# Re-planned start of a two-stage kernel: wide fillers, weights between the first units, paired score matmuls, VectorE kept off GpSimd's time

## The chip, the cores and the metric

The kernel runs on one NeuronCore of a Trainium2 chip. The metric is the device time of one execution in microseconds. It has TensorE (PE; its weight loads are listed apart as PEld), VectorE (DVE), ScalarE (ACT), GpSimd (POOL) and SyncE (SP), which issues nearly all DMAs here. A tensor of up to 128 partitions is worked on at a time; matmul results go to PSUM, which has eight banks.

## What is computed

The reference is a linear attention with a decaying state, followed by a two-layer network:

```python
for t in range(S):                       # B, H, S, D = 4, 8, 768, 48
    cur = einsum('bhd,bhe->bhde', u * k[t], v[t])
    y[t] = einsum('bhd,bhde->bhe', r[t], state + cur)
    state = w * state + einsum('bhd,bhe->bhde', k[t], v[t])
x = y as (3072, 384)                     # tokens x (heads * head size)
h = x @ w_in                             # 384 -> 2048
g = where(h >= 1, h, where(h <= -1, 0, (h + 1)**2 / 4))
out = g @ w_out                          # 2048 -> 384, float32
```

All inputs and the output are float32. The kernel computes g as the square (h/2 + 1/2)^2 alone, and finds from norms of x and of the columns of w_in whether any h could leave -1..1; a flag then sends it into a slower branch, which the given inputs do not take.

## The kernel before, in words

The time axis is cut into 6 chunks of 128 steps. One chunk of one batch is a **unit**: 24 units, chunk by chunk, so that units 0 to 3 are the first chunk of the four batches and need no earlier state. Each unit goes through these steps (lines of the kernel before):

- three loads K, R, Vf of 192 KB (L383, issued by SP);
- K and R times powers of the decay, to bfloat16 (`kw` L447, `rw` L451), and V to bfloat16 (`v`);
- a transpose: for units 0 to 7 eight matmuls (`tr` L469, or four and four as `trk` and `trr` for units 0 and 1) and a copy out of PSUM (`rk`), for the others a transposing DMA (`trd` L488);
- scores: eight matmuls into two PSUM banks (`at` L499) and two masked copies on VectorE (`mask` L505);
- the diagonal term: `P`, `dg`, `dc` for units 0 to 7, or `ku` on GpSimd and `red`; then `vd`;
- `y` L556 and L559, the sum `x` on VectorE (L571), its transpose to xT (`xp` L581 and `xt`, or `xtd` by DMA), and the sum of squares `x2` (L597);
- the state: `st` on TensorE (L607), `t`, `tw`, `bd`.

Two units make a **block** m of 256 tokens, 12 in all. Layer 1 of a block is eight pieces `L1_m_n` (six matmuls of 256 columns, L644), each ended by a ScalarE square `g` (L656) into a bfloat16 tile; layer 2 of a unit is four pieces `L2_i_s` (four matmuls of 384 columns, L667), an evacuation and a store (L690). Piece s of layer 2 needs the s-th quarter of w_out; pieces of layer 2 follow one another strictly, and so do those of layer 1. The weights come as four quarters of w_in (I0 to I3) and four of w_out (O0 to O3), 768 KB each (L419), every one converted to bfloat16 in slices that VectorE, ScalarE and GpSimd share.

The order on each engine is not written by hand. Every operation is handed to a planner (class `Plan`) with its cost on each allowed engine, what it depends on, which buffers it takes, and a due time; `run` plays them through and emits each engine's instructions in the resulting order. On the chip an engine works its list in order and waits at its head. Due times are made of a list per block (`CFG["due"]`, `CFG["step"]`) and a bias per kind. `CFG["order"]` gives the order of the first loads. Where TensorE has nothing else before a set time, the planner lets it run **fillers** `wm` (L357): two matmuls of 128 columns on zeros.

The attention part shares four PSUM banks (pool "a"), layer 1 has two ("h"), layer 2 two ("o").

Of the kernel before, what the change touches and what calls it, by code (L numbers as in the profile page):

```python
# [14 lines left out]
SEM = 0.06  # L15
CFG = {
    "order": "U0 U1 U2 U3 I0 I1 I2 I3 O0 O1 O2 U4 O3 U5 U6 U7",
    "soft": 8,
    "sw": False,
    "due": [12.12, 22.15, 27.93, 36.84, 35.31],  # L20
    "step": 12.04,
    "warm": 24.0,
    "steady": 45.0,
    "slack": 0.19,
    "split": 2,
    "bias": {
        "at": 1.0, "bd": -4.91, "c_uw": 1.38, "dg": 0.1, "ku": -0.0, "kw": 1.96, "ldVf": 1.45, "red": -0.75,
        "rk": 0.3, "rkk": -6.72, "rkr": -0.29, "rw": 1.99, "st": 0.57, "t": -0.92, "trd": 0.24, "trk": -2.87,
        "trr": -3.35, "tw": -0.9, "v": -0.89, "x2": -1.05, "xt": 2.62, "y": -2.02,
# [4 lines left out]
class Buf:  # L34
    def __init__(self, pool):
        self.pool, self.users, self.slot, self.t = pool, [], None, None


class Op:
    def __init__(self, name, engs, fn, deps, uses, allocs, due, dma, after, nb, late):  # L40
        self.name, self.engs, self.fn, self.due, self.dma = name, engs, fn, due, dma
        self.after, self.nb, self.late = [a for a in after if a], nb, late
        self.deps, self.uses, self.allocs = [d for d in deps if d], list(uses), list(allocs)
        self.eng = self.start = self.end = None
        for b in self.uses + self.allocs:
            b.users.append(self)


class Plan:
# [13 lines left out]
    def place(self, o):  # L63
        got, t = [], 0.0
        for b in o.allocs:
            best = None
            for i, cur in enumerate(self.slots[b.pool]):
                if any(g[0] == b.pool and g[1] == i for g in got):
                    continue
                if cur is None:  # L70
                    free = 0.0
                elif all(u.start is not None for u in cur.users):
                    free = max(u.end for u in cur.users) + SEM
                else:
                    continue
                if best is None or free < best[0]:
                    best = (free, i)
            if best is None:
                return None
            got.append((b.pool, best[1]))  # L80
            t = max(t, best[0])
        return t, got

    def run(self):
# [5 lines left out]
        while todo:  # L90
            cand, gone = [], []
            for o in todo:
                if any(d.start is None for d in o.deps) or any(a.start is None for a in o.after):
                    if o.late is not None and free["PE"] > o.late:
                        gone.append(o)
                    continue
# [15 lines left out]
            for o in gone:  # L112
                todo.remove(o)
                for b in o.uses:
                    b.users.remove(o)
            if not cand and gone:
                continue
            if not cand:
                raise RuntimeError("no operation can be placed: " + ", ".join(o.name for o in todo[:12]))
# [16 lines left out]
            occ, lat = o.engs[e]  # L136
            o.eng, o.start = e, est
            for b, (p, i) in zip(o.allocs, pl):
                b.slot = i
                self.slots[p][i] = b  # L140
            if o.dma is not None:
# [4 lines left out]
                begin = max(served, issue + wait)  # L146
                served = begin + took
                ring.append((served, nd))
                free[e] = issue
                o.end = served + 0.6 + (1.0 if est > steady else 0.0)  # L150
# [7 lines left out]
            todo.remove(o)  # L158
            done.append(o)
        done.sort(key=lambda o: o.start)  # L160
# [27 lines left out]
def kernel(  # L188
# [28 lines left out]
    NS = CFG["soft"]  # L217
    D_m = list(CFG["due"])
    while len(D_m) < NB + 2:
# [11 lines left out]
        "x": 5, "x2": 2, "g": 5, "os": 3, "sq": 2, "ss": 2,  # L231
    }
    P = Plan(slots)
    rows = rot.tile([1, 2, H, DP], F32, name="rows", tag=f"g_{slots['g'] - 1}")

# [15 lines left out]
    u_row = const.tile([1, H * D], F32, name="u_row")  # L251
    zero = const.tile([128, 128], BF16, name="zero")
    onesf = const.tile([1, 128], F32, name="onesf")
    w_row = const.tile([1, H * D], F32, name="w_row")
    wc = const.tile([128, NP], F32, name="wc")
    ident = const.tile([128, 128], BF16, name="ident")
    umask = const.tile([128, 128], F32, name="umask")
    ones = const.tile([128, 1], BF16, name="ones")
# [9 lines left out]
    xT = [const.tile([128, nKb, MT], BF16, name=f"xT{m}") for m in range(NB)]  # L268
    xn = const.tile([128, NU], F32, name="xn")
    wsq = const.tile([128, nN], F32, name="wsq")  # L270
# [7 lines left out]
    wc3 = wc[:, :, None].to_broadcast([128, NP, D])  # L278
    umask4 = umask[:, None, :].to_broadcast([128, NP, 128])
# [14 lines left out]
    c_wr = P.op("c_wr", {"ACT": (0.4, 0)}, lambda e: nc.scalar.dma_start(out=w_row, in_=row(w)), due=-100, dma=(0.05, 1, 0.6))  # L294
    c_ur = P.op("c_ur", {"ACT": (0.4, 0)}, lambda e: nc.scalar.dma_start(out=u_row, in_=row(u)), after=[c_wr], due=-99.5, dma=(0.05, 1, 0.6))
    c_ubc = P.op("c_ubc", {"SP": (0.4, 0)}, lambda e: nc.sync.dma_start(out=u_bc, in_=row_bcast(u)), due=D_m[NS // UB] - 25, dma=(0.7, 8, 0.6))
# [21 lines left out]
    c_um = P.op("c_um", {"POOL": (0.6, 0.7)}, f_um, due=-97)  # L318
# [8 lines left out]
    c_lrow = P.op("c_lrow", act(384, False), lambda e: nc.scalar.activation(rows[:, 0, :, 0:D], heads(w_row), AF.Ln), deps=[c_wr, c_rz], due=-98)  # L327
    c_urow = P.op("c_urow", dve(384), lambda e: nc.vector.tensor_mul(rows[:, 1, :, 0:D], heads(w_row), heads(u_row)), deps=[c_wr, c_ur, c_rz], due=8.5)
    lwb = Buf("a")

    def f_lwb(e):
        get(lwb, [128, H, D], F32)
        mm(lwb.t, onesf, rows[:, 0, :, 0:D], start=True, stop=True)
    c_lw = P.op("c_lw", pe(1.3), f_lwb, deps=[c_lrow, c_z], allocs=[lwb], due=-98)
    colb = Buf("a")

    def f_colT(e):
        get(colb, [128, 2, NP], F32)
        for i in range(2):
            for p in range(NP):  # L340
                nc.tensor.transpose(colb.t[:, i, p : p + 1], rows[:, i, 2 * p : 2 * p + 2, :].rearrange("q h d -> q (h d)"), onesf[:, 0:1])
    c_colT = P.op("c_colT", pe(0.5), f_colT, deps=[c_lrow, c_urow], allocs=[colb], due=9)
    c_wc = P.op("c_wc", {"ACT": (0.15, 0.2)}, lambda e: nc.scalar.activation(wc, colb.t[:, 0, :], AF.Exp, scale=float(C)), deps=[c_colT], uses=[colb], due=10)

    def f_uw(e):
        for s in range(2):
            nc.vector.tensor_copy(uw[halves[s], :, s], colb.t[halves[s], 1, :])
    c_uw = P.op("c_uw", {"DVE": (0.3, 0.35)}, f_uw, deps=[c_colT, c_z], uses=[colb], due=9)
# [3 lines left out]
    for i in range(160):  # L352
        def f_wm(e, i=i):
            if wmb.t is None:
                get(wmb, [128, 128], F32)
            for _ in range(2):
                mm(wmb.t, zero, zero, start=True, stop=True, skip_group_check=True)  # L357
        wm0 = P.op(f"wm{i}", pe(0.22 if i < 18 else 0.11), f_wm, deps=[c_z], uses=[wmb] if i else [], allocs=[] if i else [wmb], after=[wm0] if i else [], due=2000.0, late=CFG["warm"] if i else None)
    c_winv = P.op("c_winv", act(384), lambda e: nc.scalar.activation(Winv, lwb.t, AF.Exp, scale=negj_col), deps=[c_lw, c_icol], uses=[lwb], due=-97)
# [453 lines left out]
```

## Time and profile before

| | |
|---|---|
| median of 9 runs | 182.01 us (180.2 to 183.54) |
| the profiled execution | 180.22 us, of which its span is 178.2 us |
| TensorE busy | 168.0 us (94%) |
| VectorE, ScalarE, GpSimd busy | 111.3, 116.1, 105.1 us |
| first piece of layer 1 begins | 18.48 us |
| last quarter of w_out converted, first piece that needs it | 36.95, 37.00 us |
| last matmul ends | 172.30 us |
| DMA | 31.50 MB, mean 177 GB/s over the span |

The page cuts the span into 40 slices of 4.455 us; a digit is the busy share in tenths. Matmuls are pipelined, so the duration of a matmul is longer than the room that it takes; the distance from the start of one group to the start of the next tells that room where TensorE is never idle. Times inside the span count from its start.

### The profile page before, as it was taken

Reading aid. Unit: us, or ns where it says so; the run is one execution under the profiler, and the core shown is the slowest. Engines: PE = TensorE matmul, PEld = TensorE weight load, DVE = VectorE, ACT = ScalarE, POOL = GpSimd, SP = SyncE. Lnnn points to the kernel's source line nnn. Section 1 sums busy time; section 2 is a strip of 40 time slices with the busy share of each in tenths; the row PEclk is TensorE's granted clock in tenths of the full one; section 3 lists DMA queues with packets and bytes.
Section 4 is the critical chain, followed back from the end, with each engine's and each line's share of the span. In section 5 each row is a group of like instructions: output and inputs, shape, how many; then the busy total and the mean of one; then the engine's idle time right before and its main releaser. Section 6 shows DMA issues by size and latency. Waiting matters only on the chain.

```text
span 178.2 us, 4705 instructions
## 1 busy us (share of the span) xinstructions
PE 168.0 (94%) x1808; PEld 127.0 (71%) x1808; DVE 111.3 (62%) x221; ACT 116.1 (65%) x257; POOL 105.1 (59%) x142
## 2 busy tenths in 40 slices
PE   7899959999999999999999999999999999999960
PEld 7689947867768777777777777777767777777730
DVE  6799955399899796678667865757676444100000
ACT  4359967744756986875886885967685556554510
POOL 8658563187895999796599669579775600000000
PEclk9999999999999999999999999999999999999996
DMA  5999999999989968969979989799898962111111
GB/s 113 209 174 283 394 349 340 264 179 196 179 193 186 207 133 171 218 142 206 188 166 168 204 173 197 197 181 216 162 188 157 241 167 70 22 44 48 44 60 45
DMA packets 105920, 31.50 MB, mean 177 GB/s; under 512 B 98978, under 2 KB 104356, under 8 KB 105892
## 3 DMA queue, kind: packets, MB, share of 16 engines
q1 hardware_dynamic: 105744, 31.04, 79.6%
q8 instruction: 16, 0.26, 0.6%
q14 instruction: 12, 0.10, 0.2%
q10 hardware_dynamic: 148, 0.10, 0.2%
HBM read 20.65 MB, written 4.72 MB: 142 GB/s over the span
## 4 chain that ended last, share of the span: by engine, by line
PE 72%; DMA 11%; SPq 8%; DVE 4%; issue 1%; POOL 1%; ACT 0%; ACTq 0%; DVEq 0%
PE o L667 33%; PE h L644 29%; DMA wf<-in_moe_w_out_dram 11%; SPq L383 6%; PE a L499 3%; SPq L419 3%; PE a L559 2%; PE a L556 2%; PE a L607 1%; DVE AT L505 1%; POOL w_out_sb L284 1%; DVE x L571 1%; PE a L469 1%; DVE VD L546 0%; PE a L581 0%
## 5 line engine op out<-in xcount | busy, mean ns | idle before, releaser
L644 PE MATMUL h<-xT,w_in_sb 128*128 128x256 bf16 x576 | 77.8, 273 | 1.8 <-DVE w_in_sb L284 1.4
L667 PE MATMUL o<-w_out_sb,g 128*128 128x384 bf16 x384 | 77.0, 326 | 0.2 <-POOL w_out_sb L284 0.2
L656 ACT ACTIVATE g<-h 128x512 bf16<-128x512 f32 x96 | 56.6, 595 | 28.3 <-PE h L644 27.1
L644 PEld LDWEIGHTS <-w_in_sb 128*128 128x128 bf16 x576 | 54.4, 98 | 15.6 <-DVE w_in_sb L284 1.6
L667 PEld LDWEIGHTS <-g 128*128 128x128 bf16 x384 | 35.2, 98 | 15.8 <-issue 0.2
L505 DVE TENSOR_TENSOR AT<-a,umask 128x512 bf16<-128x512 f32 x48 | 31.1, 684 | 7.6 <-PE a L499 7.4
L546 POOL TENSOR_TENSOR VD<-V,dg 128x384 f32<-128x384 bf16 x18 | 15.7, 873 | 12.1 <-DVE dg L541 6.3
L571 DVE TENSOR_TENSOR x<-a,VD 128x384 bf16<-128x384 f32 x24 | 13.3, 554 | 12.0 <-PE a L559 10.5
L536 POOL TENSOR_TENSOR KU<-KU,R 128x384 f32<-128x384 f32 x16 | 17.7, 1109 | 3.6 <-DMA R<-in_r_dram 2.5
L451 DVE TENSOR_TENSOR KR<-R,Wpow 128x384 bf16<-128x384 f32 x20 | 17.6, 879 | 3.3 <-DMA R<-in_r_dram 3.3
L535 POOL TENSOR_TENSOR KU<-K,u_bc 128x384 f32<-128x384 f32 x16 | 18.4, 1150 | 0.1
L597 ACT ACTIVATE x<-x 128x384 bf16<-128x384 bf16 x24 | 12.5, 522 | 5.4 <-DVE x L571 5.1
L284 DVE COPY os<-o 128x384 f32<-128x384 f32 (+1 forms) x6 | 3.1, 523 | 20.3 <-ACT os L284 18.7
L618 POOL TENSOR_TENSOR T<-T,wc 128x192 f32<-128x192 f32 x20 | 11.9, 596 | 5.0 <-ACT T L284 3.6
L357 PE MATMUL o<-zero 128*128 128x128 bf16 x156 | 13.0, 236 | 1.0 <-DVE zero L321 1.0
L447 POOL TENSOR_TENSOR KR<-K,Winv 128x384 bf16<-128x384 f32 x11 | 11.0, 997 | 3.6 <-DMA K<-in_k_dram 2.8
L284 ACT COPY os<-o 128x384 f32<-128x384 f32 (+1 forms) x19 | 8.9, 469 | 6.3 <-PE o L667 4.0
L614 DVE TENSOR_TENSOR T<-T,a 48x192 f32<-48x192 f32 x32 | 11.1, 348 | 2.3 <-PE a L607 1.7
L284 ACT CAST V<-Vf 128x384 bf16<-128x384 f32 x19 | 9.6, 507 | 4.1 <-DMA Vf<-in_v_dram 3.9
L284 ACT CAST Tbd<-T 48x192 bf16<-48x192 f32 x30 | 10.4, 347 | 2.0 <-PE a L556 1.2
L357 PEld LDWEIGHTS <-zero 128*128 128x128 bf16 x156 | 10.6, 107 | 1.2 <-DVE zero L321 1.0
L447 DVE TENSOR_TENSOR KR<-K,Winv 128x384 bf16<-128x384 f32 x13 | 9.5, 727 | 2.5 <-DMA K<-in_k_dram 2.4
(78 smaller groups left out, 173.1 us busy)
## 6 DMA issues: line engine op xcount, KB each, us to landing
K<-in_k_dram SPq DMA_DIRECT2D x24, 192.0 KB, 3.8
R<-in_r_dram SPq DMA_DIRECT2D x24, 192.0 KB, 4.4
Vf<-in_v_dram SPq DMA_DIRECT2D x24, 192.0 KB, 4.2
out_dram<-os SPq DMA_DIRECT2D x23, 192.0 KB, 2.4
wf<-in_moe_w_in_dram SPq DMA_DIRECT2D x4, 768.0 KB, 8.5
wf<-in_moe_w_out_dram SPq DMA_DIRECT2D x4, 768.0 KB, 8.5
RK<-KR SPq DMA_TRANSPOSE x16, 3.2
xT<-x SPq DMA_TRANSPOSE x16, 3.1
```

The lines of the kernel that those rows point to most:

```text
L284: (nc.scalar.copy if eng == "ACT" else V_ENG[eng].tensor_copy)(o, i)
L357: mm(wmb.t, zero, zero, start=True, stop=True, skip_group_check=True)
L447: V_ENG[e].tensor_mul(krb.t[:, H:, 0:D], Kb.t, Winv)
L451: V_ENG[e].tensor_mul(krb.t[:, :H, 0:D], Rb.t, Wpow)
L505: nc.vector.tensor_mul(atb.t[s], at_p[s].t, umask4)
L535: nc.gpsimd.tensor_mul(kub.t, Kb.t, u3)
L536: nc.gpsimd.tensor_mul(kub.t, kub.t, Rb.t)
L546: V_ENG[e].tensor_mul(vdb.t, vb.t, dgb.t[:, :, None].to_broadcast([128, H, D]))
L571: nc.vector.tensor_add(xb.t, yb.t[:, 0:384].rearrange("p (h d) -> p h d", h=H), vdb.t)
L644: mm(hb.t[:, f, :], w_in_sb[:, kk, (2 * n + f) * 128 : (2 * n + f + 1) * 128], xT[m][:, kk, :], start=(kk == 0), stop=(kk == nKb - 1),)
L656: nc.scalar.activation(gb[m].t[:, 2 * n : 2 * n + 2, :], hb.t, AF.Square, bias=0.5, scale=0.5)
L667: mm(ob.t, gb[m].t[:, f, j * C : (j + 1) * C], w_out_sb[:, f, :], start=(f == 0), stop=(f == nN - 1))
```

## The change

The planner's order of the first loads, its model and several operations change; the mathematics does not.

- **Loads.** I0 now comes after unit 0's K and R and I1 after unit 1's; w_out's first three quarters are no longer mixed with unit 4's loads. The row w is loaded first, on SP's queue.
- **Decay tables.** w is spread over 128 partitions by two matmuls and then taken to its logarithm; before, the logarithm came first.
- **Fillers.** One matmul of 256 columns in place of two of 128.
- **Planner.** Matmuls that start before 9.0 us are counted twice as long; some VectorE operations are made to wait, in the plan, for GpSimd; all biases and due times are new.
- **Blocks 0 and 1.** Layer 1 works on one unit (128 columns) at a time, twelve matmuls in a piece, so that a piece needs only its own unit's xT.
- **Units.** Units 0 to 3 transpose in two halves (`split`), units 8 and 9 transpose by TensorE too, `at` of both units of a block is one operation of 16 matmuls from block 5 on, one mask of units 0 and 1 goes through ScalarE, and units 0 and 1 may use all PSUM pools.
- **Norms of w_in.** One matmul group at the end in place of eight small ones; one buffer for the squares in place of two.
- **End.** The last unit's layer 2 is 256 columns and then 128 in a PSUM bank of its own, each stored from SP; some stores of units 12 to 17 are split in two so that the number of DMAs is a multiple of 8. The branch that is not taken becomes a loop.

```diff
-    "order": "U0 U1 U2 U3 I0 I1 I2 I3 O0 O1 O2 U4 O3 U5 U6 U7",
-    "soft": 8,
+    "order": "U0 I0 U1 I1 U2 U3 I2 I3 O0 O1 O2 U4 O3 U5 U6 U7",
+    "tpe": 10, "dmm": 8, "xpe": 8, "pair": 5, "cold": 9.0, "fine": 2,
+    "am0": 0, "am1": 2, "norm": 100.0, "wide": 2,
...
+            if e == "DVE" and o.sb and free["POOL"] > est + 0.15:
+                occ, lat = occ + free["POOL"] - est - 0.15, lat + free["POOL"] - est - 0.15
+            if e == "PE" and est < CFG["cold"] and o.name[:2] != "wm":
+                occ, lat = 2.0 * occ, lat + occ
...
-        "x": 5, "x2": 2, "g": 5, "os": 3, "sq": 2, "ss": 2,
+        "x": 5, "x2": 2, "g": 5, "os": 3, "sq": 1, "ss": 2, "am": 2,
...
+    c_wr = P.op("c_wr", {"SP": (0.5, 0)}, lambda e: nc.sync.dma_start(out=w_sp[0:128:64, :], in_=w.rearrange("(s h) d -> s (h d)", s=2)), due=-1000, dma=(0.05, 1, 0.5))
...
+    def f_wb(e):
+        for s in range(2):
+            get(wbb[s], [128, H // 2, D], F32)
+            mm(wbb[s].t, onesf[s * DP : s * DP + 1, :], w_sp[s * DP : s * DP + 1, :], start=True, stop=True)
+    def f_lw(e):
+        for s in range(2):
+            nc.scalar.activation(lw[:, lws[s]], wbb[s].t, AF.Ln)
...
-            for _ in range(2):
-                mm(wmb.t, zero, zero, start=True, stop=True, skip_group_check=True)
+            mm(wmb.t, zero[:, 0:128], zero, start=True, stop=True, skip_group_check=True)
...
+        A = "a h o" if i < CFG["wide"] else "a"
+        by_pe, by_mm, x_pe = i < CFG["tpe"], i < CFG["dmm"], i < CFG["xpe"]
...
+                def f_am(e, s=s, amb=amb):
+                    get(amb, [128, NP, 128], BF16)
+                    nc.scalar.copy(amb.t, at_p[s].t)
...
+    for m in range(NB):
+        gens = [attention(UB * m + j) for j in range(UB)]
+        got = [next(g) for g in gens]
+        if m >= CFG["pair"]:
+            def f_at2(e, got=got):
+                for x in got:
+                    x[0](e)
+            o = P.op(f"at_{m}", pe(0.63), f_at2, deps=got[0][1] + got[1][1], uses=[x[2] for x in got], allocs=got[0][3] + got[1][3], due=got[0][4])
...
+            if fine:
+                get(hb, [128, 4, C], F32)
+                parts = [(f, 4 * q + f, slice(j * C, (j + 1) * C)) for f in range(4)]
...
-        parts = [(0, d_out)] if i < NU - 1 else [(0, d_out // 2), (d_out // 2, d_out)]
+        cuts = [(0, d_out)] if i < NU - 1 else [(0, 256), (256, d_out)]
+        rows_ = [(0, C)] if i not in TWICE else [(0, C // 2), (C // 2, C)]
+        for q, (lo, hi) in enumerate(cuts):
+            ob = Buf("o")
...
+    def f_np(e):
+        get(npb, [128, nP], F32)
+        for g in range(nP):
+            mm(npb.t[:, g : g + 1], mx[g], ones, start=True, stop=True)
```

## The prediction

> **What bounds the kernel now.** I read the page's 40 slices first, then the chain in order of time, then sums over stages, then the start and the end of the timeline.
>
> ```profile
> PE   7899959999999999999999999999999999999960
> DMA  5999999999989968969979989799898962111111
> ```
>
> The DMA engines are full from the second microsecond to about the eighth slice (35 us); TensorE is full to the end of slice 38, but up to 18.48 us mostly with fillers. The chain says what held it meanwhile:
>
> ```profile
> 15.98 19.75 DMA wf<-in_moe_w_out_dram x2
> ...
> 35.78 1.18 POOL w_out_sb L284 x2
> ...
> 37.00 0.81 PE o L667 x4
> ...
> 62.34 0.33 PE a L499 x8
> 62.67 0.76 PE o L667 x4
> 63.42 0.66 PE h L644 x6
> ...
> 168.39 3.91 PE o L667 x24
> ...
> 172.72 0.36 DVE os L284
> ```
>
> To 37.00 us the chain is a transfer: the last quarter of w_out, landed at 35.73 us, converted by GpSimd to 36.96, and then the first piece of layer 2 that needs it (`L2_0_3`). All later pieces of layer 2 stand behind this one. From there it is TensorE alone. The columns of the next view are the stage, its length, the busy time (instructions) of PE, PEld, DVE, ACT and POOL, the granted clock, the DMA share and GB/s:
>
> ```profile
> 30.00:36.00 6.00, 5.97 (x56) 4.84 (x53) 2.73 (x6) 4.62 (x9) 1.61 (x3) 1.00 1.06 259
> 60.00:80.00 20.00, 20.00 (x217) 14.95 (x214) 15.00 (x28) 15.90 (x38) 17.99 (x22) 1.00 0.86 170
> ```
>
> So there are three stages: to 37.00 us a gate made by DMA, with TensorE full just ahead of it too; 135.30 us of TensorE to 172.30; and a tail of 5.9 us to 178.2. The time is the gate, the work behind it, and the tail.
>
> **Work behind the gate.** The room that a group takes in a busy stretch is the distance of its start to the next start (medians over 53 to 172 us, except `tr` and `dg`, over 18 to 53): a piece of layer 1 0.655 us, of layer 2 0.650, `at` 0.33 and 0.11 more for the piece after it (0.76 above for 0.65), `y` 0.205 and 0.17 for its state part, `st` 0.17, `tr` 0.447, `xp` 0.17, `dg` 0.11, `np` 0.054. Behind `L2_0_3` the kernel before has 80 pieces of layer 1 (52.4), 93 of layer 2 (60.5), 19 `at` (8.4), 20 `y` (7.5), 16 `st` (2.7), 3 `tr` (1.3), 4 `xp` (0.7), and 1.1 for `dg`, `np` and the flag: 134.5, against 135.3 measured. It loses 0.8 us. There is next to nothing to win there by a better order.
>
> The changed order has the same pieces behind the same gate. What differs: units 8 and 9 transpose on TensorE, 2 x 0.447 = +0.9; seven pairs of `at` save one switch each, 7 x 0.11 = -0.8; `np` in one group -0.2 (eight single columns, bounded by 0.054 x 8 and nothing); the last unit in 256 and 128 columns: 16 x 0.109 (a sixth of a piece of layer 1) + 16 x 0.056 (an eighth of `tr`) = 2.64 against 2.60. Sum again 134.5.
>
> **The gate.** The early start is real. The first piece of layer 1 now needs unit 0 alone. In ScalarE's list its xT stands behind the conversion of I1, so: the first load before landed at 3.60 us, the row w ahead of it costs one issue on SP (0.5; the first two took 0.45 and 0.57), and small loads landed 1.0 us apart (3.60 to 10.61 over seven), quarters of weights 2.15 (2.11 and 2.16); I1 lands at 4.1 + 4 x 1.0 + 2 x 2.15 = 12.4, then `cI12` 0.62, `am` about 0.6 (as `g`, 0.595) and `xt` 0.48: 14.2 us in place of 18.48. But what it starts is 16 pieces of layer 1 and three of layer 2, all there is to do without O3. And O3 has the same loads ahead of it as before: twelve of units 0 to 3, K and R of unit 4, seven quarters. Moving weights between them moves no byte out of the way. By that spacing O3 lands at 3.6 + 13 x 1.0 + 8 x 2.15 = 33.8, measured 35.73; the change adds 0.5 and may get back what was lost at 12 to 14 us, where the DMA share was 0.79. The gate lies between 35.6 (spacing kept throughout) and 37.5 (the old surplus and the 0.5). TensorE sets a second gate: `L2_0_2` needs O2, which now comes one small load earlier, and after it stand four pieces of layer 1, `tr` and `at`: 33.67 - 0.5 + 0.65 + 4 x 0.67 + 0.45 + 0.44 = 37.4. I take **37.2** for 37.0. Thinner pieces (twelve of 128 columns, 0.67) and colder fillers fall before it and cost nothing as long as it holds.
>
> **VectorE and GpSimd.** The contention is there:
>
> ```profile
> 5.90 1.00 POOL L447 TENSOR_TENSOR KR<-K,Winv 128x384 bf16<-128x384 f32 x1 [0.80 <-ACT Winv L359]
> 6.04 1.27 DVE L447 TENSOR_TENSOR KR<-K,Winv 128x384 bf16<-128x384 f32 x1
> ...
> 9.55 0.55 DVE L447 TENSOR_TENSOR KR<-K,Winv 128x384 bf16<-128x384 f32 x1
> ```
>
> The same product takes 1.27 us beside GpSimd and 0.55 alone. Unit 0 gets both its products on VectorE, some 0.7 us sooner each. Behind the gate VectorE is busy 15.0 of 20 us and TensorE does not wait for it, so separating them there is worth nothing. The Trainium skill (SBUF — State Buffer, Who interferes with whom) says that a VectorE instruction with two SBUF inputs contends with GpSimd reads, and that issue order decides who blocks; the rows agree on VectorE's side. By that rule GpSimd is held as well, and a plan that delays VectorE alone covers one half; the sum is the same, GpSimd being idle 2 to 5 us of each 20 behind the gate.
>
> **The tail.** Now the two halves of the last evacuation run one after the other (172.37 + 0.32, then 172.72 + 0.36), and the last store is issued at 173.10, lands 3.40 us later and is followed by 1.7 us of closing waits, four of them (0.07 each) on lanes after the last store's. With the first part in a bank of its own only 128 columns are left: 0.07 + 0.30 + 0.02 + 3.3 + 1.4 = 5.1 us in place of 5.9. Bounds: 4.9 with a faster landing, 5.9 if the store decides alone.
>
> **The sum.** 37.2 + 134.5 + 0.8 + 5.1 = 177.6 us of span, against 178.2; outside it 2.0 us, so 179.6 against the profiled 180.22. That execution is at the fast end of the nine runs (median 182.01); moving both alike, by -0.6, gives **181.4 us**. A difference under 1%, 1.8 us, is about what cannot be told from none in this kernel.
>
> **Rivals.**
>
> *The gate opens early (faster, 0.30).* If weights mixed into small loads keep the queue full, the gate is at 35.6, the order loses 0.4, the tail is 4.9: 175.4, that is 2.8 us less, 179.2 on the median. For it: TensorE had no slack ahead of the gate before (5.97 of 6.00) and would have some, so scatter at the start (the nine runs lie up to 3.3 us above the best) would reach the end less. Against: `L2_0_2` and its four pieces hold 37.4 unless O2 is early too.
>
> *The first units pay for the weights (slower, 0.23).* R of unit 3 is now behind I0 and I1, landing at 4.1 + 10 x 1.0 + 2 x 2.15 = 18.4 us, and VectorE's list has conversions among unit 3's steps: `rkr3` behind I2, `xt2` behind I3, `xt3` behind O0. With I3 at 23.7 and O0 at 25.9 by the same count, `xt3` is done at 25.9 + 0.05 + 0.35 + 0.36 = 26.7; with the 1.9 us that O3 was late before, at 28.6. After it TensorE has seven pieces of layer 1, two of layer 2, `tr` and `at` to do, 4.7 + 1.3 + 0.9 = 6.9 us, so it decides from 37.2 - 6.9 = 30.3 us on, and each microsecond past that is one at the end. At 33.5 us, five late, the end moves by 3.2: 184.6. What could do it is one weight landing 3.3 us after the other, as I2 did after I1 (20.06, 23.37), in front of such a conversion.
>
> A rule speaks for it: the Trainium skill (TensorE: Matmul & The Clock Gate, What's actually happening) has the array at half clock until a window of about 3.4 us was busy, and again after an idle one. Before, 28 fillers took 3.17 us at the start (113 ns each) and 16 later 1.07 (67 ns), so the first part is seen here; a fall back is not. With half the filler time between the first units, by the rule seven pieces at double length would add 7 x 0.67 = 4.7 us, of which the slack ahead of the gate takes some.
>
> *The rest (0.47)* is the forecast. In it sits what a pair of `at` could cost: it takes all four banks of pool "a", and the even unit's `y` follows after 2.0 us of TensorE work, where two masks (2 x 0.68) and the step between engines need 1.45 and one VectorE product in front up to 0.7. If each of seven pairs lost 0.2 us, the end would move by 1.4.
>
> **Range.** 178.8 to 184.6: the fast case with its bounds (gate 35.6, tail 4.9, loss none) and the slow one at its price. The chances are those of the cases: 0.30 faster, 0.47 within 1%, 0.23 slower.
>
> **What would show it.** The first layer-1 piece near 14 us; O3 landing at 34.3 to 36.2 and `L2_0_3` starting at 36 to 37.5; `xt3` before 30; from there to the last matmul 135 to 136 us; last matmul to the end 5.1. A gate at 39 or later, TensorE idle in the stages from 40 to 140, or the last quarter landing at 33 would make the prediction wrong.

## The result, and the profile after

The changed kernel is slower: **184.54 us** median (182.76 to 186.58, 20 runs) against 181.18 of the kernel before (62 runs), a ratio of **1.0215**, 95% interval 1.0192 to 1.0239. Its profiled execution has a span of 182.5 us, against 178.2. The ratios leave out, as disturbed, runs more than 1.5% above the fastest of the same kernel (in the comparison of the runs called h, 12 of 19 of the kernel before), and one profile below (j1) is of such a run, so that only its tail is read.

Cut as the prediction cut it, the 4.3 us of span are:

| | before | predicted | after |
|---|---|---|---|
| first piece of layer 1 | 18.48 | 14.2 | 15.90 |
| gate: `L2_0_3` begins | 37.00 | 37.2 | 40.17 |
| from there to the last matmul | 135.3 | 135.3 | 138.1 |
| last matmul to the end | 5.9 | 5.1 | 4.2 |

Both rows that were to stay as they were grew, by 3.2 and 2.8 us; the end gained 1.7. The page's slices of the changed kernel (4.56 us each) show the busy share in tenths:

```profile
PE   7989886969999899999999999979999998999990
DMA  4999899889799965996996978997976973311111
```

TensorE has holes in the seventh and ninth slices (27 to 32 and 36 to 41 us), and again at about 60, 120 and 150 us, where it had none before. The chain in order of time (start, duration, what) names them:

```profile
20.53 18.20 DMA wf<-in_moe_w_out_dram x2
38.78 0.57 POOL w_out_sb L318
39.42 0.70 POOL w_out_sb L318
40.17 0.81 PE o L749 x4
...
113.40 5.67 DMA Vf<-in_v_dram
119.09 0.52 ACT V L318
119.66 0.33 PE a L657 x4
...
139.73 3.00 DMA K<-in_k_dram
...
148.42 3.32 DMA RK<-KR
151.79 0.40 PE a L535 x8
```

The gate is still w_out's last quarter, O3, but it landed at about 38.75 us in place of 35.73. Behind it the chain is no longer TensorE alone: it goes back to the loads of a V and a K and to a transpose by DMA. In the view of waits (total, times, longest) the changed kernel's TensorE has

```profile
PE o L749 <- POOL w_out_sb L318: 1.5, 1, 1.5
PE a L657 <- ACT V L318: 1.5, 1, 1.5
...
PE a L535 <- DMA RK<-KR: 1.1, 2, 0.8
...
PE a L631 <- DVE x L621: 0.7, 1, 0.7
```

and the kernel before, from its gate to its last matmul, only

```profile
PE o L667 <- POOL w_out_sb L284: 0.2, 1, 0.2
PE a L581 <- DVE AT L505: 0.2, 1, 0.2
```

The last three of the changed kernel are its loss behind the gate. Measured as the distance between two matmuls' starts less the room that the first takes, they are 1.60 us at 119.7 (V of unit 17), 0.44 at 140.3 and 1.00 at 151.8 (second unit of a pair), 0.95 at 60.0 (x of unit 7): 4.0 in sum, where the stretch is 3.6 longer than the 134.5 of work that the prediction counted. Before, no distance behind the gate exceeds its room by more than 0.4 us. This measure is used below as "stall".

Why O3 is late shows in the DMA columns of two stretches of time. The row is the stretch, its length, PE, PEld, DVE, ACT, POOL, the clock, the DMA share and GB/s; first before, then after:

```profile
18.00:20.00 2.00, 2.00 (x41) 1.78 (x38) 1.89 (x5) 1.93 (x7) 0.90 (x2) 1.00 1.06 393
33.00:35.00 2.00, 2.00 (x19) 1.59 (x18) 1.07 (x3) 1.35 (x3) 0.38 (x1) 1.00 1.20 266
```

```profile
18.00:20.00 2.00, 1.48 (x24) 1.00 (x21) 1.41 (x4) 1.93 (x5) 0.51 (x1) 1.00 0.58 92
33.00:35.00 2.00, 1.92 (x29) 1.60 (x27) 1.56 (x4) 1.55 (x3) 0.69 (x1) 1.00 0.61 78
```

(A share above 1 means that the times of packets overlap.) The DMA engines run dry twice while there is plenty left to load. In both places a weight is issued behind two or more small loads (I2 at 16.46 behind K3 to R3, O3 at 29.79 behind K4 and R4), with another weight ahead of these. Most of O3's delay is such idle time: counted from the packets in the two traces (packets under way over 16 engines, at most 1), the engines stood idle for 3.6 us until O3 had landed before, and for 6.2 in the changed kernel. Of these 2.7 us, 0.7 lie ahead of 4 us, 1.0 between 16 and 24 and 1.2 behind 32; from 4 to 16 us the changed kernel has 0.2 less.

### The profile page after: what moved, and what is told of

Same layout as the page of the kernel before. It is cut to its first block, busy times and chain, and to the rows that moved or that the text cites. A ratio compares the mean times of both kernels' runs of the same rounds, so it can differ in the third digit from the quotient of the medians.

```text
span 182.5 us, 4715 instructions
## 1 busy us (share of the span) xinstructions
PE 167.9 (92%) x1820; PEld 127.6 (70%) x1820; DVE 111.5 (61%) x221; ACT 119.6 (66%) x265; POOL 100.3 (55%) x143
## 4 chain that ended last, share of the span: by engine, by line
PE 62%; DMA 20%; DVE 6%; POOL 3%; issue 2%; ACT 2%; SPq 2%; POOLq 0%; DVEq 0%; ACTq 0%
PE o L749 28%; PE h L715 23%; DMA wf<-in_moe_w_out_dram 10%; DMA wf<-in_moe_w_in_dram 3%; DMA Vf<-in_v_dram 3%; PE a L535 2%; DMA RK<-KR 2%; PE a L657 2%; PE a L609 2%; DMA K<-in_k_dram 2%; DVE AT L553 1%; PE a L606 1%; PE o L403 1%; PE a L505 1%; DVE P L565 1%
## 5 line engine op out<-in xcount | busy, mean ns | idle before, releaser
L715 PE MATMUL h<-xTa,w_in_sb 128*128 128x256 bf16 (+1 forms) x672 | 77.9, 257 | 2.4 <-ACT g L728 1.4
L749 PE MATMUL o<-w_out_sb,g 128*128 128x384 bf16 (+2 forms) x400 | 76.4, 319 | 1.5 <-POOL w_out_sb L318 1.5
L715 PEld LDWEIGHTS <-w_in_sb 128*128 128x128 bf16 x672 | 56.7, 98 | 15.0 <-issue 1.8
L730 ACT ACTIVATE g<-h 128x512 bf16<-128x512 f32 x80 | 47.6, 595 | 29.7 <-PE h L715 28.8
L553 DVE TENSOR_TENSOR AT<-a,umask 128x512 bf16<-128x512 f32 x45 | 28.4, 683 | 12.8 <-PE a L535 12.8
L487 DVE TENSOR_TENSOR KR<-R,Wpow 128x384 bf16<-128x384 f32 x24 | 18.7, 779 | 4.3 <-DMA R<-in_r_dram 4.3
L668 POOL TENSOR_TENSOR T<-T,wc 128x192 f32<-128x192 f32 x20 | 12.4, 627 | 11.5 <-ACT T L318 5.9
L318 ACT COPY os<-o 128x384 f32<-128x384 f32 (+2 forms) x19 | 8.8, 461 | 6.2 <-PE o L749 5.7
L318 DVE COPY os<-o 128x384 f32<-128x384 f32 x6 | 3.3, 558 | 14.8 <-PE o L749 14.6
L800 POOL TENSOR_TENSOR ss<-sq 128x256 bf16<-128x256 bf16 x8 | 5.3, 667 | 12.5 <-ACT sq L791 12.5
L591 DVE TENSOR_REDUCE dg<-KU 128x8 f32<-128x384 f32 x16 | 8.6, 546 | 5.7 <-POOL KU L586 5.7
L403 PE MATMUL o<-zero 128*128 128x256 bf16 x46 | 10.7, 369 | 1.1 <-DVE zero L356 1.1
```

The costliest lines, as they stand in the source:

```text
L318: (nc.scalar.copy if eng == "ACT" else V_ENG[eng].tensor_copy)(o, i)
L403: mm(wmb.t, zero[:, 0:128], zero, start=True, stop=True, skip_group_check=True)
L487: V_ENG[e].tensor_mul(krb.t[:, :H, 0:D], Rb.t, Wpow)
L553: nc.vector.tensor_mul(atb.t[s], at_p[s].t, umask4)
L715: mm(hb.t[:, f, :], w_in_sb[:, kk, c * 128 : (c + 1) * 128], xT[m][:, kk, cols], start=(kk == 0), stop=(kk == nKb - 1))
L730: nc.scalar.activation(gb[m].t[:, 2 * n : 2 * n + 2, :], hb.t, AF.Square, bias=0.5, scale=0.5)
```

## The experiments

Two things are asked: does the order of the loads make the gate late, and through what; and what makes TensorE stand behind the gate. In edits, `x>y` means that operation x is set right behind y in the planner's finished list, all else staying. The table has each run's profiled execution and its ratio to before in the same comparison.

| run | `L2_0_3` | behind | tail | span | ratio (95%) |
|---|---|---|---|---|---|
| before | 37.00 | 135.3 | 5.9 | 178.2 | |
| after | 40.17 | 138.1 | 4.2 | 182.5 | 1.0215 (1.0192 to 1.0239) |
| g1 K4 early | 38.99 | 136.4 | 4.7 | 180.1 | 1.0145 (1.0095 to 1.0195) |
| g2 before, new order | 40.88 | 136.4 | 5.2 | 182.5 | 1.0234 (1.0155 to 1.0313) |
| g3 after, old order | 37.00 | 137.4 | 4.4 | 178.9 | 1.0048 (1.0010 to 1.0086) |
| g4 w by ScalarE | 38.97 | 136.5 | 4.4 | 179.8 | 1.0133 (1.0025 to 1.0242) |
| h1 g3, V early | 36.90 | 137.3 | 4.1 | 178.3 | 1.0095 (1.0048 to 1.0143) |
| h2 g3, whole stores | 37.26 | 136.0 | 4.2 | 177.5 | 1.0012 (0.9945 to 1.0079) |
| h3 g3, at apart | 37.04 | 137.1 | 4.7 | 178.8 | 1.0149 (0.9958 to 1.0340) |
| h4 g3, w by ScalarE | 37.50 | 136.8 | 4.0 | 178.4 | 1.0103 (0.9920 to 1.0287) |
| i1 h2 + V early + dg4 | 37.91 | 136.4 | 4.5 | 178.8 | 0.9977 (0.9947 to 1.0007) |
| i2 after, whole stores | 40.07 | 136.2 | 4.2 | 180.4 | 1.0103 (1.0041 to 1.0165) |
| i3 before, split stores | 36.48 | 139.3 | 6.6 | 182.4 | 1.0107 (1.0046 to 1.0169) |
| i4 K4, R4 by ScalarE | 40.82 | 137.0 | 4.5 | 182.3 | 1.0178 (1.0111 to 1.0246) |
| j1 before, new end | | | 4.5 | | 0.9932 (0.9873 to 0.9991) |
| j2 h2, no pairs | 37.01 | 136.3 | 4.1 | 177.3 | 0.9999 (0.9960 to 1.0039) |
| j3 h2, stores by ScalarE | 37.32 | 135.1 | 4.1 | 176.5 | **0.9946** (0.9911 to 0.9981) |
| k1 j3, xp7 later | 37.09 | 134.8 | 4.8 | 176.7 | **0.9901** (0.9864 to 0.9938) |
| k2 j1, stores by ScalarE | 36.26 | 137.1 | 5.3 | 178.6 | 0.9991 (0.9951 to 1.0031) |

### The gate

**g1**, one load moved (`ldK4>ldO0`):

> The changed kernel, every engine's list as it was, but the load K of unit 4 is issued right behind O0 and no longer behind O2, so that only R of unit 4 stands directly ahead of O3. **Theory 'room'**: SP's issue of a load blocks until the queue has room for its pieces, and a small load (1024 runs of 192 bytes) takes more of that room than a quarter of weights (384 or 512 runs) for a quarter of the bytes. K4 and R4 together fill the queue with few bytes, O3 is issued only when O2 is nearly through (issue over at 33.12, 33.42 landed), and the engines run dry (busy share 0.28 in microsecond 33). With K4 away O3's issue is over by 31.5, it lands at 36.9 (36.3 to 37.5) in place of 38.75, the first piece that needs it starts at 38.3 in place of 40.17, the span goes from 182.5 to 180.6 and the ratio to before from 1.0215 to about 1.011. **Rival 'late start'**: the queue lost its time at the start (first load 0.86 us later, dips at 8 to 11 us); the same bytes lie ahead of O3, it lands at 38.4 to 38.9 and the span stays within 0.5 of 182.5. **Rival 'first units'**: O3 lands early but TensorE, busy with the first blocks, still reaches that piece at 40.

O3's first conversion began at 36.95 in place of 38.75, as 'room' said. SP's issues (start, duration) show how; first the changed kernel, then g1:

```profile
23.10 1.66 SPq L427 DMA_DIRECT2D K<-in_k_dram  x1
24.80 4.83 SPq L427 DMA_DIRECT2D R<-in_r_dram  x1
29.79 3.33 SPq L454 DMA_DIRECT2D wf<-in_moe_w_out_dram  x1
```

```profile
22.57 3.50 SPq L454 DMA_DIRECT2D wf<-in_moe_w_out_dram  x2
26.12 2.18 SPq L427 DMA_DIRECT2D R<-in_r_dram  x1
28.46 1.50 SPq L454 DMA_DIRECT2D wf<-in_moe_w_out_dram  x1
```

An issue that takes 0.5 us when the queue is short took 4.83 here, and ended (29.63) as O0 landed (29.13); O3's ended (33.12) as O2 was about to land (33.42). In g1 both are shorter and the busy share at 33 to 35 us is 1.09. The kernel before had such an issue too (the first of these two, O1, took 5.10 us), but with no gap in the transfers behind it, and its O3 went out at 27.45:

```profile
18.91 6.91 SPq L419 DMA_DIRECT2D wf<-in_moe_w_out_dram  x2
25.86 1.47 SPq L383 DMA_DIRECT2D R<-in_r_dram  x1
27.45 1.34 SPq L419 DMA_DIRECT2D wf<-in_moe_w_out_dram  x1
```

But in g1 the gate came only to 38.99, in place of the 38.3 of 'room', and TensorE was busy for all of the 4 us ahead of it: there a second bound is met, as the third expectation had it. The span fell 2.4 us, 1.2 of it at the gate. The rest lies behind the gate (136.4, with no stall for V of unit 17), which the theory did not reckon with; that the span comes near the expected 180.6 is in part luck.

**g2**, the kernel before with SP's first 24 loads in the changed order:

> The kernel before, every engine's list as it was, but SP issues its first 24 loads in the order of the changed kernel (I0 behind R0, I1 behind R1, I2 behind R3, K4 and R4 together ahead of O3). Nothing else of the change is in it. **Room**: the order alone makes the gate late: O3 lands at 37.9 to 38.8 (35.73 before), the piece that needs it starts at 39.3 to 40.2, and since the lists are not planned for this order the first units may lose something more; ratio 1.013 to 1.03. **Late start** (w first on SP, which is not in here): O3 stays within 0.5 of 35.7 and the ratio is 1.00 to 1.005.

The time is as slow as expected and the way is not. O3's conversion began at 36.73, only 1.0 later; but the other engines' lists, planned for the old order, stood behind it: the first piece of layer 1 came at 24.01 and the conversions of O3 ended at 41.2. So it shows that the order costs this without the rest of the change, on lists planned for another order, not that O3's landing alone is the cause.

**g3**, the changed kernel planned again with the old order (one line of `CFG`):

```diff
-    "order": "U0 I0 U1 I1 U2 U3 I2 I3 O0 O1 O2 U4 O3 U5 U6 U7",
+    "order": "U0 U1 U2 U3 I0 I1 I2 I3 O0 O1 O2 U4 O3 U5 U6 U7",
```

> The changed kernel, planned again with the load order of before (units 0 to 3 ahead of I0 to I3); all other parts of the change stay, w first on SP among them. **Room**: O3 lands at 36.0 to 37.0 and the piece that needs it starts at 37.4 to 38.4, although the first piece of layer 1 goes back from 15.9 to 18 or later; behind the gate the stalls of the changed kernel (V, the last pairs of at) may be placed otherwise, 135.5 to 138.1 us; ratio 1.000 to 1.015. **Late start**: O3 at 37.8 or later, the gate 39 or later.

This settles it for the gate (the planner made every list anew, so that not SP's alone differs): O3 landed at 35.94, the gate is at 37.00, the same as before the change, although layer 1 began at 19.04 and not at 15.90 and w still went first. Of 2.15% only 0.48% is left. The early start was worth nothing, and its price was the gate.

**g4** (w by ScalarE's queue) and **i4** (K4 and R4 by ScalarE's queue):

> The changed kernel with the row w loaded through ScalarE's queue, as in the kernel before, so that K0 is the first issue on SP; every list otherwise as it was. **Room**: the first load lands about 0.8 us earlier (3.7 in place of 4.46), but O3's issue waits for room at 33 us as before, so O3 lands 0 to 0.4 us earlier and the span is 182.1 to 182.5. **Late start**: all landings move by 0.7 to 0.8, O3 to 38.0, the span to 181.7.

O3's conversion began at 37.55, 1.2 earlier, more than either gave. 'Room' was wrong to expect that nothing moves: room comes when something lands, and all that lay ahead (O2: 32.34 in place of 33.42) landed earlier. The ratio's interval takes in that of the changed kernel, so what w costs is not settled.

> The changed kernel with its load order, but K and R of unit 4 are issued by ScalarE's queue (at the place of its list that the order of issue gives) and no longer by SP ahead of O3. Bytes and their order of issue stay about as they were. **Room**: the room that held O3 back belongs to SP's queue; O3's issue is over by 27 (33.12 in the changed kernel), there is no gap at 33 to 35 us, O3 lands at 35.5 to 37.0, and the piece that needs it starts at 38.4 to 39.2, where TensorE's own list takes over as in g1; span 180.3 to 181.3. **Rival 'bytes'**: the engines had no faster way for these loads in any queue; O3 lands at 38 or later.

The gap is gone (share 1.10 at 33 to 35 us, 0.61 in the changed kernel) and O3 was issued at 24.84, but it began to be converted only at 37.84, between the two expectations. O0 to O2 now landed 3.18 and 2.86 us apart (2.05 and 2.24 in the changed kernel), beside the other queue's loads and the ones that SP was free to issue next; R4 landed at 38.15 and TensorE stood 0.4 us for it, and with O2 late too (35.03 in place of 33.42) the gate came to 40.82. So the room that held O3 back belongs to SP's queue, but here more room brought no more bandwidth.

### Behind the gate

With the old order, three edits of the finished list were tried first.

**h1**, `ldVf16>xtd12 ldVf17>ldVf16`:

> The changed kernel with the load order of before (as g3), every list as there, but the loads of V of units 16 and 17 are issued by SP three to six places earlier: ahead of a transpose of x, one of K and R, K17, a store and R17. **Theory 'late on SP'**: the stalls behind the gate come from loads and transposes that stand in SP's list behind other waiting instructions; there V17 landed at 115.25 and the state matmuls that need it stood for 1.08 us (0.34 us more for V16). With both earlier these two stalls go and the span falls from 178.9 to 177.5 (177.2 to 178.2), or a part is given back, as K17 and the transposes behind come 1.2 us later. **Rival 'VectorE and ScalarE full'**: V's conversion on ScalarE was late, not its load; the stall stays above 0.7 us.

The stalls at V16 and V17 went, so the late load was their cause. But 137.3 us behind the gate is 137.4 again: this execution stood 0.95 us for unit 7's x and 0.82 and 0.41 us at 101 us around another unit's state, both ahead of the place of the edit. Such small stalls come and go between executions, which a single profile can't tell from a cause.

**h3**, the second unit's `at` two pieces later in blocks 10 and 11:

> As g3, every list as there, but in the last two pairs (blocks 10 and 11) the second unit's eight score matmuls stand two pieces of layers 1 and 2 behind the first unit's, and no longer directly behind them. **Theory 'pair'**: the pair makes the first half's order rigid, TensorE stands idle inside it for the second unit's RK while pieces of the layers are ready; apart, these pieces fill the time: the stalls of 0.58 and 0.83 us go, two switches of 0.11 come back, span 178.9 to 177.7. **Rival 'late unit'**: unit 21 and 23 are late anyhow; the idle time appears at their y or at the next block's first piece instead, the span stays at 178.5 to 179.2.

The stalls inside the pairs went and one of 1.09 us came at 148 us, at layer 1, for a transpose of x issued by SP; the span stayed at 178.8, as the rival had it. It is not the pair that costs the time. That SP is late is tried next.

**h4** (w by ScalarE's queue, with the old order):

> As g3, with the row w through ScalarE's queue as in the kernel before, so that K0 is SP's first issue. In g3 the DMA engines had no gap between 3 and 35 us. **Theory**: with the queue full throughout, a start 0.7 us earlier carries through: O3 lands at 35.2 to 35.6 in place of 35.94, the piece that needs it starts at 36.3 to 36.7 in place of 37.00, the span is 178.2 to 178.6. **Rival**: the early time is lost again, as small loads that come earlier are not faster (about 185 GB/s at a busy share of 1.4 in g3 between 8 and 13 us); O3 stays at 35.7 to 36.1.

O3 landed at 35.12, even earlier than the theory had it, but its conversion took 2.2 us (35.18 to 37.38) and the gate came to 37.50, not to 36.3 to 36.7: nothing won that can be measured.

**h2**, whole stores:

```diff
-                def fo(e, lo=lo, hi=hi, r0=r0, r1=r1):
-                    nc.sync.dma_start(out=out[t0 + r0 : t0 + r1, lo:hi], in_=osb.t[r0:r1, lo:hi])
+                def fo(e, lo=lo, hi=hi, r0=0, r1=C, k=k):
+                    if k == 0: nc.sync.dma_start(out=out[t0 + r0 : t0 + r1, lo:hi], in_=osb.t[r0:r1, lo:hi])
```

> As g3, every list as there, but the stores of units 12 to 17 are one each again and not two halves (six issues of about 0.6 us less on SP, between 119 and 148 us). **Late on SP**: what stands behind them, loads of the last units and their transposes, is issued 0.6 to 1.2 us earlier, and the stalls in the last two pairs of at (0.58 and 0.83 us, second unit's RK) shrink to 0.1 to 0.5 in sum; the span falls by 0.7 to 1.2, to 178.0. **Rival 'norms on GpSimd'**: the transposes wait for kw behind the norm sums on GpSimd; both stalls stay as they are.

Both stalls in the pairs are gone, 136.0 us in place of 137.4; the medians of all runs are 179.49 us against 180.81 of the kernel before. The interval of its ratio overlaps that of g3, so the same edit was made without the old order (**i2**), and its reverse in the kernel before (**i3**):

> The changed kernel as it is, with its own load order, but whole stores for units 12 to 17. **Theory**: the gate stays at 40.2 (39.9 to 40.4), the two stalls in the pairs of at (0.44 and 1.00 us in the changed kernel) fall to 0.3 or less in sum, behind the gate 136.6 to 137.2 in place of 138.1; span 181.0 to 181.7, ratio about 1.013. **Rival**: the split stores cost nothing by themselves and h2's gain was scatter: behind the gate 137.8 or more, span 182 or more.

> The kernel before, every list as it was, but the stores of units 12 to 17 are issued in two halves each, as in the changed kernel. **Theory 'late on SP'**: SP loses 0.6 us six times between 115 and 150 us. In before nothing waits for SP there (no stall above 0.25 us), so the split alone costs 0 to 0.5 us, ratio 0.998 to 1.004; it takes the late loads and the paired at of the changed order to make it 1.4. **Rival 'stores by themselves'**: the halves cost what they cost there, 1 to 1.5 us, ratio 1.006 to 1.009, with stalls at transposed RK behind 130 us.

i2 went the way expected and further: behind the gate 136.2 in place of 138.1 (136.6 to 137.2 expected), with the gate where it was, and the two intervals of the ratio don't touch. In i3 my theory fell and the rival held, its price a little low: six stores in halves cost the kernel before 1.07% by themselves. SP's issues there, first in i3, then before:

```profile
141.46 1.34 SPq L488 DMA_TRANSPOSE RK<-KR  x1
142.90 2.46 SPq L691 DMA_DIRECT2D out_dram<-os  x4
145.45 1.23 SPq L589 DMA_TRANSPOSE xT<-x  x1
146.79 1.25 SPq L488 DMA_TRANSPOSE RK<-KR  x1
```

```profile
138.68 1.36 SPq L488 DMA_TRANSPOSE RK<-KR  x1
140.13 1.03 SPq L690 DMA_DIRECT2D out_dram<-os  x2
141.25 1.20 SPq L589 DMA_TRANSPOSE xT<-x  x1
142.56 1.25 SPq L488 DMA_TRANSPOSE RK<-KR  x1
```

Half a store takes SP as long as a whole one (0.58 against 0.55 us), the last transpose is issued 4.2 us later (in part because this execution, the slowest of i3's four, had lost time ahead of the split stores too), and TensorE, which had not stood for a transpose in this part before, stood for the last two:

```profile
PE a L499 <- DMA RK<-KR: 1.8, 2, 0.9
```

How near SP is to its limit is a number that the page doesn't give, since issuing isn't counted as busy: the durations of SP's DMA issues fill 18.3 of the 20 us from 100 to 120 and 22.9 of the 25 to 145 in the kernel before, 18.7 and 23.1 in the changed one. By this measure SP is the fullest engine but TensorE. The sum is no measure of the loss, though: some of it is time spent blocked, and in i2, with whole stores, it is 18.7 and 23.0. What the six issues cost is what i2 and i3 measured.

**j3** moves ten stores off it (the stores of units 8 to 17 on `nc.scalar`, in h2):

> As h2, with the whole stores of units 8 to 17 issued by ScalarE and no longer by SP. SP's issues fill 18.5 of 20 us there (100 to 120 us) and 22.5 of 25 (120 to 145); ten stores of 0.55 us or more leave it. **Theory 'SP is full'**: loads and transposes come earlier, V17's stall (1.17 us) shrinks to below 0.3, behind the gate 134.6 to 135.2, span 176.3 to 177.0. **Rival 'ScalarE pays'**: each store stops ScalarE for 0.5 us or until VectorE's evacuation is done, the squares of layer 1 come late, TensorE waits at layer 1 or 2; behind the gate 136.5 or more.

SP falls from 18.6 to 16.3 of 20 us and from 23.1 to 18.8 of 25, V17 is issued at 108.72 in place of 110.29 in h2, and its stall is gone; behind the gate 135.1 us, as 'SP is full' expected. 178.88 us median against 181.02: faster than both kernels. Against h2, the intervals of the two ratios still overlap.

**i1**, **j2**, **j1**, **k1** and **k2** ask what else there is.

> The changed kernel with what the runs so far point to: the load order of before (as g3), whole stores for units 12 to 17 (as h2), V of units 16 and 17 loaded earlier (as h1), and the diagonal matmuls of unit 4 (dg4) one piece of layer 2 later, as TensorE stood 0.77 us for them right behind the gate in g3 and h2. **Theory**: gate 36.9 to 37.4, behind it 134.3 to 135.2 (136.0 in h2, less 1.2 for V17 and 0.6 for dg4), tail 4.2: span 175.6 to 176.7, against 178.2 of the profiled kernel before; ratio 0.982 to 0.992. **Rival 'stalls move'**: what no longer waits for V17 or dg4 waits for the next late thing (x of unit 7, the last transposes); behind the gate 135.8 or more, span 177.2 or more, ratio 0.995 or above.

V17 and dg4 no longer stall and others do (0.94 us at 99 for a transpose), behind the gate 136.4: the rival.

> The changed kernel with the load order of before and whole stores (as h2), planned again without pairs of at: every unit's scores stand alone in TensorE's list. **Theory 'pairs are worth 0.8'**: seven switches of 0.11 come back; with no stall at pairs left in h2 (0 above 0.24 us), behind the gate it takes 136.6 to 137.0 in place of 136.0. **Rival 'pairs bring the stalls'**: single units need less at one time, V17's stall of 1.17 us goes with them, and behind the gate it takes 134.8 to 135.6.

136.3 against 136.0 and the same ratio within the intervals: neither expectation. Both had a part in it. The stall for V17 did go: stalls above 0.25 us sum to 0.9 us in j2 and 2.1 in h2. And yet j2 takes 0.3 longer, so that it has 1.5 us more of work: the seven switches are 0.8 of it, the rest stays open. In the sum pairs gain nothing that can be measured, and bring no loss.

> The kernel before with one part of the change alone: the last unit's layer 2 in 256 and then 128 columns, each in a PSUM bank of its own and each stored from SP. Everything up to it is planned as before. **Theory**: the end is the part that gains: last matmul to end 4.2 to 4.9 us in place of 5.93, work behind the gate 135.3 as before; span 176.8 to 177.5, ratio 0.992 to 0.996. **Rival 'last store decides'**: the last store's landing and the closing waits take what they took; tail 5.6 or more, ratio 0.998 to 1.002, and the short tails of the changed kernels come from the even number of transfers or from the other branch.

The tail is 4.5 us in place of 5.9: the new end is the part of the change that shortens it. The three profiles with the old end (before, g2, i3) have tails of 5.2 to 6.6 us, the sixteen with the new one 4.0 to 5.3. How much of it is gained in time is less sure: the interval ends just below one, and the medians of all runs are 180.81 and 181.02 us.

> As j3 (the changed kernel with the load order of before, whole stores, those of units 8 to 17 issued by ScalarE), with one step moved: the transpose of unit 7's x on TensorE stands one piece of layer 2 (and st of unit 8) later, as TensorE stood 0.95 us for that x at 57 us. **Theory**: 0.7 to 0.95 us of it go, behind the gate 134.2 to 134.6, span 175.6 to 176.0; ratio 0.988 to 0.992. **Rival**: the first piece of layer 1 of that block, which needs this xT, now waits instead; span 176.3 to 176.8, ratio 0.993 to 0.996 as j3.

The stall at unit 7's x is gone and one of 0.45 us is left behind it; behind the gate 134.8. The span is that of j3 (the tail was 0.7 longer), the ratio 0.9901 overlaps j3's, so the step itself is not shown to gain. As a whole k1 has the lowest ratio here, 178.91 us against 181.31, and from its gate to its last matmul its view of waits has as little left as that of the kernel before:

```profile
PE o L749 <- POOL w_out_sb L318: 0.2, 1, 0.2
PE a L535 <- DVE RK L318: 0.2, 1, 0.2
```

> The kernel before with two things alone: the new end (as j1) and the stores of units 8 to 17 issued by ScalarE (as j3). **Theory 'SP is full in before too'**: the small stalls for transposed K and R and for V that before shows in some executions (j1: 0.68, 0.61, 0.40, 0.42 us) go, behind the gate 134.6 to 135.2, tail 4.2 to 4.6, span 175.8 to 176.8, ratio 0.984 to 0.992. **Rival 'before has room'**: its order has nothing waiting on SP; behind the gate 135.2 to 136, and only the end gains: ratio 0.992 to 0.997.

Neither expectation: with the new end (tail 5.3) and ten stores off SP, the kernel before gained nothing that can be measured (0.9991), and 0.77, 0.58 and 0.70 us for transposes and V were seen in its profile, 137.1 behind the gate. So issues on SP are shown as the cause of what the split stores cost, in both orders; that moving whole stores off SP gains is seen in the changed kernel's lists alone (j3, V17), and that SP also bounds the kernel before is not shown.

## Why the prediction was wrong

- **"Moving weights between them moves no byte out of the way"** is the step that failed. True of the bytes, it was used as if bytes were all that a queue counts. What the runs showed in its place: SP's issue blocks (up to 4.83 us) when small loads stand in the queue behind a weight. A small load (1024 runs of 192 bytes) seems to hold more of the queue's room than a quarter of weights (384 or 512 runs, four times the bytes); the next weight goes out late, and the engines run dry (0.58 and 0.61 of their time busy in two stretches). O3 landed 3.0 us late and the gate opened at 40.17, outside the bounds of 35.6 to 37.5, whose upper end held only the old surplus and the one issue of w. g3 shows that the order is the cause; g1 shows K4's place as a part of it, and i4 that the room is that of SP's queue. How much room a load takes was not measured by itself. The planner in both kernels has a guess at it: there an issue waits while more than 160 pieces would be under way, of which a small load counts for 64 and a quarter of weights for 24 or 32. The prediction used neither that nor the blocked issues in the profile of the kernel before.
- **The first piece of layer 1** missed its 14.2 in part in the same way: SP issued I1 only at 8.52, because R1's issue ahead of it stood for 3.78 us, and ScalarE began I1's conversion at 13.94, where 12.4 was reckoned.
- **The second gate, 37.4**, was the right thought with one wrong term: it was worked out from `L2_0_2` at 33.17, half a microsecond earlier than before. O2 landed at 33.42 in place of 32.62, `L2_0_2` began at 34.43, `at` of unit 4 stood at 38.30, and g1, with O3 early, ran into 38.99: there `L2_0_2` began at 34.79 and the work behind it took 4.20 us, as reckoned (4.22). That TensorE would have slack ahead of the gate by starting earlier (the faster rival) was wrong too: layer 2 began at 30.88 in place of 28.91, as the weights behind the first units came later.
- **"The changed order has the same pieces behind the same gate"** counted TensorE's pieces and assumed the loss of 0.8 to stay. The split stores were in the diff and were not in the sum: six more issues on SP, 0.58 us each, priced by i2 at 1.9 us in the trace and 1.1% of the time. VectorE and GpSimd were checked for room and SP was not. Nor does "TensorE does not wait for it", read off VectorE before, hold for the changed order: it stood 0.95 us at 60.0 for x of unit 7, which VectorE makes.
- **Pairs** (-0.8 and up to 1.4 of loss): taking them out changed nothing that can be measured (j2). The stalls at pairs were the split stores' (gone in h2 and i2, pairs and all).
- **The tail** went the right way and by more: 4.2 for 5.1. The last 128 columns are evacuated in 0.27 us, from 178.32 on, and j1 has 4.5 with this part alone. Two terms were too large: from the last store's issue (178.61) to the end of SP's wait for it and for TensorE (181.60) it took 3.0 in place of 3.3, and the closing waits 0.9 in place of 1.4. Before, twelve of SP's short waits (0.07 us each) came behind the last landing, and in the changed kernel one.
- **The first units** were not the way to the loss: unit 3's xT was done by 29.8, ahead of the 30.3 from which the slower rival decides. Its price, 184.6, was met by other mechanisms, so that the measured 184.54 lies inside the range by luck.
- **Fillers.** The Trainium skill (TensorE: Matmul & The Clock Gate, What's actually happening) was cited for half clock until a busy window, and for a fall back after an idle one. The first half is seen, and by more than before: in the kernel before 128-column matmuls start 107 ns apart up to 3.7 us and 56 from 5.6 on; in the changed kernel the 256-column fillers start 213 ns apart up to 13.6 us and 109 from 15.1 on, so that nearly all work ahead of layer 1 ran at half rate (the profile's granted clock is 1.00 throughout and does not show it). The first pieces of layer 1 have 56 ns from 15.9 us on; no fall back is seen. What the slow start cost was not tried by itself. It does not hold the gate: there TensorE stands 1.5 us for the conversion of O3.
- **"TensorE is full"** up to the gate passed over the sixth digit of its row, 5: between 23 and 27 us it stood 1.4 and 0.4 us for conversions of w_in. The sum does not rest on it.
- The Trainium skill (DMA: Bandwidth & Descriptors, Issuing engines are not separate DMA queues) says that issuing from several engines saves only the issuer's time, "which is usually small relative to the DMA itself". The first half agrees with i4, where a second issuer brought no bandwidth (quarters landed 3.18 and 2.86 us apart in place of 2.05 and 2.24). The second is true of one half store (0.58 us of the 2.2 to its landing) and no guide to many: six issues more on SP cost the kernel before 1.07% (i3).

Not settled: what w as SP's first issue costs (g4 and h4 have wide intervals), what the slow start of TensorE costs, and why single executions differ by a microsecond in the small stalls behind the gate.

## What to carry to other kernels

Count the issuing engine as an engine: sum the durations of its issues over a stretch, for the profile's busy part leaves them out. Where that sum is near the stretch, as here, ask what waits behind each further issue; here six split transfers were paid at the end in both kernels. Order loads by what they take of the queue's room, not by bytes alone: twice here a large load was issued late behind small ones that stood behind another large one, and the engines ran dry in between. Small loads alone did not do it: in g3 eleven of them stand ahead of I0 and the engines have no such gap from 12 to 16 us. An earlier start of work that ends at the same gate gained nothing here, and what it moved in front of the gate was its price.

## What the runs showed that was not expected

A store of half the rows costs SP as much issue time as a whole one (0.58 and 0.55 us). An issue can block for 4.8 us (5.1 in the kernel before) with the engine that issues it doing nothing else. And TensorE's branch at the end, over a loop that is not taken, lasted 3.8 us in the trace of the changed kernel (177.68 to 181.46, from 0.6 us ahead of the last matmul's end), and SP's wait of 181.60 ended just behind it. In the kernel before it lasted 3.6 us (169.82 to 173.45) and was over before the last store landed.
